# Turning rows for the gate as four-byte pairs instead of two-byte elements

## The chip, the core and the metric

The kernel runs on one core of a Trainium2 chip. The metric is the time of one execution on the device, in microseconds (us). The time before the change is 1499.75 us, the median of three runs (1499.15 to 1501.63).

## What is computed

Eight sequences of 2496 rows and 256 columns go through a Fourier transform along the rows, a complex product with a weight matrix, a soft threshold and the inverse transform. Each of the 19,968 resulting rows is then sent to the one of eight experts whose logit is largest, and the expert's output is scaled by the gate's probability. Cut to what matters:

```python
X = np.fft.rfft(x, axis=1)
Yr = Xr @ w_r - Xi @ w_i + b_r
Yi = Xr @ w_i + Xi @ w_r + b_i
Yr = np.sign(Yr) * np.maximum(np.abs(Yr) - lam, 0.0)   # Yi alike
y = np.fft.irfft(Yr + 1j * Yi, n=x.shape[1], axis=1)   # rows, 256 columns

logits = y @ w_gate                                    # 8 experts
expert_idx = np.argmax(logits, axis=1)
probs = softmax(logits)
h = np.maximum(y_sorted[lo:hi] @ w1[e], 0.0)           # per expert
out = gate_w[:, None] * (h @ w2[e])
```

## The kernel before, in words

**The transform stages.** A transform of 2496 points is split into one of 39 and one of 64 points, each a matmul with constants. For each of the eight batches: s1 (line 474) multiplies the rows of x by the first constant, and its result goes to DRAM (zd). Five groups follow: zload (line 492) brings z back, s2 (line 503) does the second transform, wmul (lines 531 to 533) the product with the weight matrix, thr and thr_sub (lines 540, 552) the threshold on VectorE, with ScalarE and GpSimd between them, inv1 (lines 579 to 581) the first half of the inverse, inv1_lo (line 591) its eviction, and vstore (line 596) the store to DRAM (vd). Nearly all products are made of two-byte halves: a value is kept as a high part and a low part in float16.

**From y to the gate.** The second half of the inverse runs on six chunks of a batch, five of four row groups and one of two. vload (line 622) brings v back, inv2 (line 632) multiplies, inv2_hi (ScalarE, line 639) and inv2_lo (VectorE, line 646) write a chunk's rows into yr: 128 rows on the partitions, and for each of four groups 256 high parts followed by 256 low parts. ytrans (VectorE, line 661) turns yr in squares of 32 by 32 elements into yt, so that columns of y come to lie on partitions. logits (TensorE, lines 674 and 676) then loads 128 columns of yt as weights, 16 times per chunk, and multiplies them with gd, the gate's weights in a block layout: the partition of gd is 32 q + i, and its block k holds the gate row that answers to the 32-wide square k. The first eight loads are of the high parts, the last eight of the low parts. route1 to route3 (from line 685) find the expert and the place of each row, and scatter (GpSimd, line 750) writes rows to their expert's list in DRAM.

**The experts.** A table (lines 854 to 909, VectorE) says which block of 256 rows is for which expert. It is made in parts as batches finish; the first part covers 12 blocks, needs batches 0 and 1 routed and all 16 weight matrices prepared (wprep, lines 768 to 807). fetch_w (lines 914, 922) and fetch_x (lines 928 to 933, with a transposing DMA) are issued on SyncE's queue, after SyncE has read the expert and the row from the table. post (lines 947, 950) reads the fetched tail on VectorE, up (lines 967 to 969) and down (lines 994 to 996) are the two matmuls of a block, down_store (line 1005) writes the result.

**What sets the order.** Every piece of work above is a task with an engine, a planned duration, a rank and dependences. A planner (class Plan) plays these through once when the program is built, and the order in which tasks start in that play is the order of the instructions on each engine's queue. Buffers of a pool are handed out in the same play. Batches 0 and 1 are routed early; from batch 2 on vload is held back to times 430, 520, ... of the play, so that the rest lies between expert blocks. Loads of expert weights for preparation are released at 40 + 26 u:

```python
ld = A("SP", 1.0, wprep_load, u, take=[wa], dma=3.4, rank=0.5, after=WT0 + WTD * u)
late = INV0 + INVD * (b - 2) if b >= 2 else 0.0
```

The planned duration of ytrans is 2.15 us for a full chunk.

Of the kernel before, what the change touches and what calls it, by code (L numbers as in the profile page):

```python
# [11 lines left out]
I32 = mybir.dt.int32  # L12
# [6 lines left out]
D = 256  # L19
# [233 lines left out]
def build(ctx: ExitStack, tc: tile.TileContext, x, w_r, w_i, b_r, b_i, wg, w1, w2,  # L253
# [3 lines left out]
    V, S, P, T, Q = nc.vector, nc.scalar, nc.gpsimd, nc.tensor, nc.sync  # L257
# [43 lines left out]
    wgs = cst.tile([128, 8, NE], F32, name="wgs")  # L301
# [17 lines left out]

    def load_g():  # L320
        for q in range(4):
            Q.dma_start(wgs[32 * q:32 * q + 32], wg.rearrange("(b i) e -> i b e", i=32))

    def load_cd():
        Q.dma_start(cd, c_d.rearrange("p (k m) -> p k m", k=K1))
# [329 lines left out]
    def ytrans(b, c):  # L655

        s = st[b]
        ns = min(4, SLOTS - 4 * c)
        yt = s[("yt", c)] = pool.tile([128, 4, 512], F16, name="yt", bufs=BUF["yt"])
        yt = s[("yt", c)] = yt.rearrange("p a b -> p (a b)").rearrange("p (k j t) -> p k j t", k=16, j=4)  # L660
        V.transpose(yt[:, :, :ns].rearrange("p k j t -> p j k t"),
                    s[("yr", c)][:, :ns, 0:2 * D].rearrange("p j (k t) -> p j k t", t=32))

    def logits(b, c):

        s = st[b]
        ns = min(4, SLOTS - 4 * c)
        yt = s.pop(("yt", c))
        o = lg[:32 * ns, c].rearrange("p h q e -> p (h q e)")
        for k in range(16):  # L670
            w = yt[:, k, :ns].rearrange("p j t -> p (j t)")
            g = gd[:, k % 8].rearrange("p h q e -> p (h q e)")
            if k < 8:
                T.matmul(o, w, g, start=(k == 0), stop=False)
            else:
                T.matmul(o[:, 0:32], w, g[:, 0:32], start=False, stop=(k == 15))
# [338 lines left out]
    A = L.add  # L1015
# [20 lines left out]
    i_w = A("SP", 1.0, load_w, rank=0, dma=1.8, take=[wu])  # L1036
    i_b = A("SP", 1.0, load_b, rank=0, dma=0.5)
    i_g = A("SP", 1.5, load_g, rank=0, dma=0.5)
    i_cd = A("SP", 0.6, load_cd, rank=0, dma=4.5)
    i_r = A("SP", 1.8, load_rest, rank=0.4, dma=2.0, after=26.0)  # L1040
# [19 lines left out]
    def ns_(c):  # L1060
        return min(4, SLOTS - 4 * c)
# [3 lines left out]
    for u in range(2 * NE):  # L1065
# [5 lines left out]
        for i in range(2):  # L1071
            m_ = A("DVE", 0.95, wprep_mul, u, i, deps=[scl], rank=1.2)
            h = A("ACT", 1.05, wprep_hi, u, i, deps=[m_], rank=1.2)
            l = A("POOL", 2.2, wprep_lo, u, i, deps=[h], rank=2, free=[wa])
# [4 lines left out]
    for b in range(B):  # L1079
# [3 lines left out]
        for c in range(6):  # L1083
            if b:
                ld.append(A("SP", 1.3, load_x, b, 4 * c, 4 * c + ns_(c), deps=[s1l[b - 1, c], nps[b - 1][c]],
                            rank=0.3, dma=8.0 * ns_(c) / 22))
# [9 lines left out]
        for c in range(6):  # L1096
            pb_, zb = L.buf("mm"), L.buf(("zt", "zt", "yt", "yt", "vs", "vs")[c] if b == 0 else "zt")
            k = ns_(c) / 4
            t = s1l[b, c] = A("PE", 1.72 * k, s1, b, c, deps=[ld[c], i_cc, nm] + ([s1l[b, c - 1]] if c else []),
                              rank=F - 9.5, take=[pb_, zb] + ([zdb] if not c else []))  # L1100
            l = A("ACT", 1.05 * k, s1_out, b, c, deps=[t], free=[pb_], rank=1)
# [3 lines left out]
        for i in range(5):  # L1105
            zs_, p2_, xa_, pw_, u_, cl_, sh_, pa_, vt_ = (L.buf(n) for n in ("zs", "mm", "xa", "mm", "u", "cl", "sh", "mm", "vt"))
            zl = A("SP", 1.2, zload, b, i, deps=sts, take=[zs_], free=[zdb], dma=11.8 / 5, rank=0)
            t = A("PE", 1.85, s2, b, i, deps=[zl, i_cd], take=[p2_, xa_], free=[zs_], rank=F + 3)
            h = A("ACT", 1.05, s2_hi, b, i, deps=[t, xs], rank=1)
            l = A("DVE", 1.28, s2_lo, b, i, deps=[h], free=[p2_], rank=1)  # L1110
            n_ = A("DVE", 0.5, s2_neg, b, i, deps=[l], rank=1)
            w = A("PE", 5.22, wmul, b, i, deps=[n_, wp_], take=[pw_, u_], free=[xa_], rank=F + 2)
# [8 lines left out]
            l = A("DVE", 1.28, inv1_lo, b, i, deps=[h], free=[pa_], rank=0)  # L1121
# [3 lines left out]
        pre = b < NPRE  # L1125
# [6 lines left out]
        for c in range(6):  # L1132
            k = ns_(c) / 4
            vs_, pb_, yr_, yt_ = (L.buf(n) for n in ("vs", "mm", "yr", "yt"))
            yrs.append(yr_)
            vl = A("SP", 0.6, vload, b, c, deps=vst + [i_z], take=[vs_], dma=9.1 * k / 5.5, rank=0.5 if pre else 2, after=late)
            t = A("PE", 1.3 * k, inv2, b, c, deps=[vl, i_r] + ([rt3["inv2", b - 1]] if b and not c else []),
                  take=[pb_, yr_], free=[vs_], rank=I + 2, lag=0.0 if pre else 6.0)
            h = A("ACT", 1.05 * k, inv2_hi, b, c, deps=[t, ys], rank=1 if pre else 1.5)
            l = A("DVE", 1.28 * k, inv2_lo, b, c, deps=[h], free=[pb_], rank=1 if pre else 1.5)  # L1140
            tks.append(A("POOL", 0.4, inv2_tok, b, c, deps=[h], rank=0.5))
            yt = A("DVE", 2.15 * k, ytrans, b, c, deps=[l], take=[yt_], rank=1 if pre else 1.4)
            lgs.append(A("PE", 0.5, logits, b, c, deps=[yt, gp_] + lgs[-1:] + ([rt3[b - 1]] if b else []), free=[yt_], rank=I + 1, lag=0.0 if pre else 2.0))
            if c == 5:
                rt3["inv2", b] = t
# [18 lines left out]
    def order(j):  # L1164

        d = [("d", j - 1, t) for t in range(2 if j <= NF else 1)] if j else []
        return [("u", j, 0)] + d + [("u", j, 1)] if j < NF else [("u", j, 0)] + d if j < NB else d
# [9 lines left out]
    for j in range(NB + 1):  # L1177
        o = order(j)
        seq += [o[i] for i in (0, 1, 3, 2)] if len(o) == 4 and j > js else o
    for j in range(NB):  # L1180
# [3 lines left out]
                       take=[xb_[j], tb_[j]], dma=1.95 if j < NF else 0.98, rank=1.2 + j * 1e-3, prev=ft.get(j - 1))  # L1184
        for w in range(2):
            wb_[j, w] = L.buf(f"wt{SLOT[j]}{w}")
            wl[j, w] = A("SP", 0.8, fetch_w, j, w, deps=[tabs[ep]] + (wdone if j < 2 else []) + ([sw] if j >= js else []),
                         take=[wb_[j, w]], dma=1.3, rank=1.1 + j * 1e-3 + w * 5e-4,
                         prev=wl.get((j - 1, w)))
    for k, (kind, j, q) in enumerate(seq):  # L1190
        if kind == "u":
# [3 lines left out]
            if q == 0:  # L1195
# [3 lines left out]
            t = ul[j, q] = A("PE", 2.65, up, j, q, deps=[ft[j], wl[j, 0], tb_["g", j][1]], take=[pb_, hb[j, q]],  # L1199
                             free=[xb_[j], wb_[j, 0]], rank=M + k)  # L1200
# [3 lines left out]
        else:  # L1204
            ob, pp = own("o", j), L.buf(f"po{q if j < NF else j % 2}")
            hs_ = [hb[j, i] for i in range(2 if j < NF else 1)]
            t = A("PE", 2.62, down, j, q, deps=[ul["o", j, i] for i in range(len(hs_))] + [wl[j, 1]], take=[pp],
                  free=hs_ + [wb_[j, 1]], rank=M + k)
# [23 lines left out]
```

## Time and profile before

| | us |
|---|---|
| median of three runs | 1499.75 |
| the profiled execution | 1501.02 |
| its span, first to last instruction | 1499.0 |
| TensorE busy in the span | 1402.3 |
| VectorE busy | 937.3 |
| ScalarE busy | 661.0 |
| GpSimd busy | 537.0 |

TensorE is PE in the rows, its weight loads PEld; VectorE is DVE, ScalarE ACT, GpSimd POOL, SyncE and its queue SP and SPq. The profiled execution is 1.3 us above the median. The mean granted clock of TensorE is 0.98 of full speed. The share of busy time is a mean over two different halves: up to about 541 us the transform stages run, after that mostly expert blocks. The table by stage in the section with the rows shows this.

### The profile page before, as it was taken

How to read it: one execution, taken by the hardware profiler on the slowest of the kernel's cores; microseconds unless marked ns; L12 is line 12 of the kernel's file. 1: busy time of each engine (PE TensorE's matmuls, PEld its weight loads, DVE VectorE, ACT ScalarE, POOL GpSimd, SP SyncE). 2: the span in 40 equal slices, each digit the busy share in tenths (PEclk: the TensorE clock that was granted, in tenths of full speed). 3: DMA queues.
4: the chain of work that ended last, by engine and by line, in shares of the span. 5: the costliest groups of instructions: out<-in, count | busy, mean ns of one | idle time of the engine just before them, and what ended most of it. 6: DMA issues, size and time to landing. Idle time of an engine off the chain costs nothing.

```text
span 1499.0 us, 33559 instructions
## 1 busy us (share of the span) xinstructions
PE 1402.3 (94%) x12850; PEld 1184.7 (79%) x12850; DVE 937.3 (63%) x1776; ACT 661.0 (44%) x869; POOL 537.0 (36%) x463
## 2 busy tenths in 40 slices
PE   5879888989887799999999999999999999999998
PEld 2668675767676578888888888888888888889997
DVE  2456788869686878666676666676666433343443
ACT  4667767766777444232333333323322222232222
POOL 0123314643564412643534525535435311111211
PEclk8999999999999899999999999999999999999999
DMA  8899978896899673874978988988678374676883
GB/s 258 246 287 290 267 231 266 254 314 177 265 289 262 176 196 81 228 197 108 308 219 249 256 240 248 226 232 239 187 228 230 81 233 115 188 201 205 213 210 104
DMA packets 229968, 330.00 MB, mean 220 GB/s; under 512 B 125109, under 2 KB 177623, under 8 KB 214960
## 3 DMA queue, kind: packets, MB, share of 16 engines
q1 hardware_dynamic: 213536, 286.78, 68.8%
q0 software_dynamic: 16272, 41.09, 8.1%
q8 instruction: 101, 1.65, 0.5%
q14 instruction: 59, 0.48, 0.1%
HBM read 276.61 MB, written 106.76 MB: 256 GB/s over the span
## 4 chain that ended last, share of the span: by engine, by line
PE 75%; DVE 9%; DMA 6%; issue 4%; ACT 3%; SPq 2%; POOL 1%; another core or an unknown queue 0%; POOLq 0%; ACTq 0%; DVEq 0%
PE pob L994 9%; PE mm L967 9%; PE pob L996 9%; PE mm L969 9%; PE mm L968 9%; PE pob L995 9%; PE mm L531 3%; PE mm L632 3%; PE mm L533 3%; PE mm L532 3%; PE mm L474 2%; DMA x<-x 2%; DVE vt L591 1%; PE mm L503 1%; DVE u L552 1%
## 5 line engine op out<-in xcount | busy, mean ns | idle before, releaser
L969 PE MATMUL mm<-xt,wt 128*128 128x256 f16 (+1 forms) x1472 | 367.0, 260 | 0.4 <-issue 0.2
L968 PE MATMUL mm<-xt,wt 128*128 128x256 f16 (+1 forms) x1472 | 367.0, 260 | 0.3 <-issue 0.3
L967 PE MATMUL mm<-xt,wt 128*128 128x256 f16 (+1 forms) x1472 | 367.1, 260 | 0.0
L1005 POOL DMA_INDIRECT out<-o,ix x163 | 176.5, 1083 | 512.5 <-ACT o L1001 415.0
L996 PE MATMUL pob<-wt,hh 128*128 128x256 f16 x1304 | 355.5, 273 | 2.1 <-issue 2.1
L994 PE MATMUL pob<-wt,hh 128*128 128x256 f16 x1304 | 355.4, 273 | 1.3 <-ACT o L1001 0.9
L995 PE MATMUL pob<-wt,hh 128*128 128x256 f16 x1304 | 355.4, 273 | 0.7 <-issue 0.7
L973 ACT ACTIVATE r<-mm 128x1024 f32<-128x1024 f32 x163 | 166.7, 1023 | 347.7 <-PE mm L969 293.4
L978 DVE CAST hh<-r 128x1024 f16<-128x1024 f32 x163 | 114.2, 700 | 252.5 <-ACT r L973 243.7
L750 POOL DMA_INDIRECT rows<-yr,ix x176 | 191.0, 1085 | 79.8 <-issue 60.7
L983 DVE TENSOR_TENSOR hh<-r,hh 128x1024 f16<-128x1024 f32 x163 | 199.8, 1226 | 5.5
L563 POOL TENSOR_TENSOR sh<-u,sh 128x1024 f16<-128x1024 f32 x40 | 86.7, 2168 | 291.3 <-ACT sh L558 283.2
L1001 ACT ACTIVATE o<-pob,g 128x256 f32<-128x256 f32 x163 | 76.4, 473 | 257.2 <-PE pob L996 248.5
L531 PE MATMUL mm<-w,xa 128*128 128x256 f16 x640 | 175.7, 275 | 9.3 <-DVE vt L591 4.6
L532 PE MATMUL mm<-w,xa 128*128 128x256 f16 x640 | 175.5, 274 | 0.0
L533 PE MATMUL mm<-w,xa 128*128 128x256 f16 x640 | 175.4, 274 | 0.0
L968 PEld LDWEIGHTS <-wt 128*128 128x128 f16 x1472 | 144.1, 98 | 15.9 <-issue 0.5
L967 PEld LDWEIGHTS <-wt 128*128 128x128 f16 x1472 | 144.0, 98 | 15.6
L969 PEld LDWEIGHTS <-wt 128*128 128x128 f16 x1472 | 144.0, 98 | 13.5 <-issue 0.5
L995 PEld LDWEIGHTS <-hh 128*128 128x128 f16 x1304 | 127.5, 98 | 17.6 <-issue 2.7
L996 PEld LDWEIGHTS <-hh 128*128 128x128 f16 x1304 | 127.5, 98 | 17.5 <-issue 2.0
L994 PEld LDWEIGHTS <-hh 128*128 128x128 f16 x1304 | 127.6, 98 | 16.4 <-issue 1.5
(172 smaller groups left out, 2073.0 us busy)
## 6 DMA issues: line engine op xcount, KB each, us to landing
wt<-wsc SPq DMA_DIRECT2D x184, 1024.0 KB
zs<-zd SPq DMA_DIRECT2D x80, 256.0 KB
vd<-vt SPq DMA_DIRECT2D x80, 256.0 KB
vs<-vd SPq DMA_DIRECT2D x40, 480.0 KB
x<-x SPq DMA_DIRECT2D x120, 156.0 KB
zd<-zt SPq DMA_DIRECT2D x37, 480.0 KB
wt<-moe_w SPq DMA_DIRECT2D x32, 512.0 KB
wsc<-wt SPq DMA_DIRECT2D x32, 512.0 KB
```

The source lines that it names most:

```text
L531: T.matmul(o, lh, w16[:, r, h, 0, :], start=(h == 0 and r == 0), stop=False)
L532: T.matmul(o, lh, w16[:, r, h, 1, :], start=False, stop=False)
L533: T.matmul(o, ll, w16[:, r, h, 0, :], start=False, stop=(h == 1 and r == 1))
L750: i = P.indirect_dma_start(out=rows, out_offset=bass.IndirectOffsetOnAxis(ap=s["ix"][:, j:j + 1], axis=0), in_=s[("yr", j // 4)][:, j % 4, ...
L967: T.matmul(pv[:, a, :], wh, xt[:, h, :], start=(h == 0), stop=False)
L968: T.matmul(pv[:, a, :], wh, xt[:, 2 + h, :], start=False, stop=False)
L969: T.matmul(pv[:, a, :], wl, xt[:, h, :], start=False, stop=(h == 1))
L983: V.tensor_tensor(hh[:, :, 1, :], H.pop(("r", j, q)).rearrange("p (a n) -> p a n", n=n), hh[:, :, 0, :], ALU.subtract)
L994: T.matmul(po, hi, wh, start=(fc == 0), stop=False)
L995: T.matmul(po, hi, wl, start=False, stop=False)
L996: T.matmul(po, lo, wh, start=False, stop=(fc == 7))
L1005: i = P.indirect_dma_start(out=out, out_offset=bass.IndirectOffsetOnAxis(ap=ix[:, t:t + 1], axis=0), in_=H.pop(("o", j, t)), in_offset=Non ...
```

## The change

The rows of y are turned as four-byte elements: two neighbours in a row, each of two bytes, stay together as one. A chunk has 1024 such elements per partition instead of 2048. After the turn, a partition of yt holds pairs, one of an even and one of an odd column of y. logits therefore takes every second element of yt as weights, the even ones for one matmul and the odd ones for the next, and the gate's rows are loaded in the order of the pairs. The planned duration of ytrans becomes 1.1 us.

```diff
     def load_g():
         for q in range(4):
-            Q.dma_start(wgs[32 * q:32 * q + 32], wg.rearrange("(b i) e -> i b e", i=32))
+            Q.dma_start(wgs[32 * q:32 * q + 32], wg.rearrange("(b i o) e -> i b o e", i=32, o=2))
...
-        yt = s[("yt", c)] = yt.rearrange("p a b -> p (a b)").rearrange("p (k j t) -> p k j t", k=16, j=4)
-        V.transpose(yt[:, :, :ns].rearrange("p k j t -> p j k t"),
-                    s[("yr", c)][:, :ns, 0:2 * D].rearrange("p j (k t) -> p j k t", t=32))
+        yt = s[("yt", c)] = yt.rearrange("p a b -> p (a b)").rearrange("p (k m o) -> p k m o", k=8, o=2)
+        V.transpose(yt.rearrange("p k m o -> p (k m o)").bitcast(I32).rearrange("p (k j t) -> p j k t", k=8, j=4)[:, :ns],
+                    s[("yr", c)][:, :ns, 0:2 * D].bitcast(I32).rearrange("p j (k t) -> p j k t", t=32))
...
         for k in range(16):
-            w = yt[:, k, :ns].rearrange("p j t -> p (j t)")
+            w = yt[:, k // 2, :32 * ns, k % 2]
             g = gd[:, k % 8].rearrange("p h q e -> p (h q e)")
...
-            yt = A("DVE", 2.15 * k, ytrans, b, c, deps=[l], take=[yt_], rank=1 if pre else 1.4)
+            yt = A("DVE", 1.1 * k, ytrans, b, c, deps=[l], take=[yt_], rank=1 if pre else 1.4)
```

The planned duration is one number, but the play goes differently from the first transposes on, and so does the order on every engine. Three places follow, each as it stands before and then after.

The first is SyncE's queue at the first expert fetch (xt and tl are a block's rows and their tails, rows the experts' lists in DRAM, zs the z of a group, vd and vs the store and load of v). Before:

```order
L931 DMA_TRANSPOSE xt_5404<-rows 128x4x256
L933 ISA
L933 DMA tl_5406<-rows 128x2x4
L928 TENSOR_LOAD tab_5298
L928 ISA x2
L931 ISA
L931 DMA_TRANSPOSE xt_5472<-rows 128x4x256
L933 ISA
L933 DMA tl_5474<-rows 128x2x4
L596 DMA vd_116<-vt 64x4x512 x2
L492 DMA zs<-zd_108 64x4x256 x2
```

After:

```order
L931 DMA_TRANSPOSE xt_5625<-rows 128x4x256
L933 ISA
L933 DMA tl_5627<-rows 128x2x4
L928 TENSOR_LOAD tab_5317
L928 ISA x2
L931 ISA
L931 DMA_TRANSPOSE xt_5658<-rows 128x4x256
L933 ISA
L933 DMA tl_5660<-rows 128x2x4
L622 DMA vs<-vd_112 120x1024
L622 DMA vs<-vd_113 120x2048
L596 DMA vd_117<-vt 64x4x512 x4
```

Ahead of the first L931 stand 76 of 80 loads of line 492 before and all 80 after; 66 of 80 stores of line 596 before and 72 after.

The second is TensorE at the first expert matmul (sm holds the logits, wt an expert's weights). Before:

```order
L676 LDWEIGHTS yt
L676 MATMUL sm<-gd,yt 128x32
L967 LDWEIGHTS wt_74
L967 MATMUL mm<-xt_5404,wt_74 128x256
L968 LDWEIGHTS wt_74
L968 MATMUL mm<-xt_5404,wt_74 128x256
```

After:

```order
L632 LDWEIGHTS cg
L632 MATMUL mm<-vs,cg 128x512
L967 LDWEIGHTS wt_74
L967 MATMUL mm<-xt_5625,wt_74 128x256
L968 LDWEIGHTS wt_74
L968 MATMUL mm<-xt_5625,wt_74 128x256
```

Ahead of the first L967 stand 304 of 320 matmuls of line 503, 576 of 640 of each of lines 531 to 533 and 140 of 160 of each of lines 579 to 581 before; after the change 320, 640 and 152.

The third is VectorE at its first expert instructions (g is made from the fetched tail tl and the table; u is the threshold's buffer). Before:

```order
L540 SCALAR_TENSOR_TENSOR u<-mm,bt 128x1024
L947 TENSOR_SCALAR g_5523<-tl_5406,tab_5298 128x2
L950 COPY ix_5525<-tl_5406 128x2
L591 SCALAR_TENSOR_TENSOR vt<-mm,vt 128x4x256
L552 SCALAR_TENSOR_TENSOR u<-u,sb,cl 128x1024
L947 TENSOR_SCALAR g_5565<-tl_5474,tab_5298 128x2
L950 COPY ix_5567<-tl_5474 128x2
L513 SCALAR_TENSOR_TENSOR xa<-mm,sb,xa 128x8x128 x2
L519 TENSOR_SCALAR xa<-xa 128x16x64 x2
L646 SCALAR_TENSOR_TENSOR yr<-mm,sb,yr 128x4x256
L661 STREAM_TRANSPOSE yt<-yr 128x4x16x32
```

After:

```order
L540 SCALAR_TENSOR_TENSOR u<-mm,bt 128x1024
L552 SCALAR_TENSOR_TENSOR u<-u,sb,cl 128x1024
L947 TENSOR_SCALAR g_5717<-tl_5627,tab_5317 128x2
L950 COPY ix_5719<-tl_5627 128x2
L513 SCALAR_TENSOR_TENSOR xa<-mm,sb,xa 128x8x128 x2
L947 TENSOR_SCALAR g_5741<-tl_5660,tab_5317 128x2
L950 COPY ix_5743<-tl_5660 128x2
L519 TENSOR_SCALAR xa<-xa 128x16x64 x2
L646 SCALAR_TENSOR_TENSOR yr<-mm,sb,yr 128x4x256
L591 SCALAR_TENSOR_TENSOR vt<-mm,vt 128x4x256
L661 STREAM_TRANSPOSE yt<-yr 128x4x8x32
```

Ahead of the first L947 stand 36 of 40 instructions of line 540 and 34 of 40 of line 591 before, 38 and 36 after.

## Rows read from the trace of the kernel before

**Rows 1.** The page: busy us, share of the span and instructions of each engine.

```profile
PE 1402.3 (94%) x12850; PEld 1184.7 (79%) x12850; DVE 937.3 (63%) x1776; ACT 661.0 (44%) x869; POOL 537.0 (36%) x463
```

**Rows 2.** Table by stage: stretch and length, busy us by engine, granted clock, DMA.

```profile
core 0: us, PE busy (x) PEld busy (x) DVE busy (x) ACT busy (x) POOL busy (x), PEclk, DMA share, GB/s
0.00:150.00 150.00, 120.51 (x778) 89.08 (x779) 71.70 (x163) 97.47 (x139) 26.32 (x17) 0.92 0.93 270
150.00:541.00 391.00, 333.95 (x2634) 258.51 (x2633) 306.95 (x536) 267.00 (x344) 172.11 (x116) 0.96 0.85 253
541.00:600.00 59.00, 58.68 (x586) 52.78 (x583) 48.13 (x92) 27.93 (x35) 13.15 (x11) 1.00 0.37 90
600.00:1100.00 500.00, 495.55 (x4755) 426.00 (x4753) 335.64 (x637) 156.62 (x201) 225.10 (x224) 1.00 0.82 225
1100.00:1499.00 399.00, 393.56 (x4110) 358.30 (x4107) 174.88 (x350) 112.00 (x151) 100.29 (x98) 1.00 0.65 182
```

**Rows 3.** VectorE by line and shape: busy us, mean ns of one, idle before.

```profile
L661 DVE STREAM_TRANSPOSE yt<-yr 128x2048 f16<-128x2048 f16 x40 | 92.3, 2309 | 1.1
L794 DVE TENSOR_SCALAR wt<-wt,wn 128x1024 f32<-128x1024 f32 x32 | 34.2, 1088 | 0.3
...
L661 DVE STREAM_TRANSPOSE yt<-yr 128x1024 f16<-128x1024 f16 x8 | 9.9, 1239 | 0.2
```

**Rows 4.** Transposes of line 661 by stage: stretch, busy us, count, clock, DMA.

```profile
150.00:541.00 391.00, 34.56 (x16) 0.96 0.85 253
...
600.00:1100.00 500.00, 64.01 (x30) 1.00 0.82 225
```

**Rows 5.** Waits from 150 to 541 us: who for whom, us, times, longest.

```profile
PE sm L601 <- ACT junk L570: 6.6, 3, 5.1
...
PE mm L531 <- DVE vt L591: 4.6, 2, 3.6
...
PE mm L579 <- issue: 0.2, 1, 0.2
...
ACT cl L546 <- DVE u L540: 34.2, 12, 7.6
```

**Rows 6.** The chain from 500 to 545 us (start, us, what), SyncE's wait, its load.

```profile
519.36 0.27 DVE tb L900
...
523.92 5.64 SPq L931
529.77 5.71 DMA tl<-rows
...
SPq L914 <- DVE tb L900: 10.1, 1, 10.1
...
535.48 2.03 SPq L492 DMA_DIRECT2D zs<-zd  x2
```

**Rows 7.** TensorE in order of time (start, us, line, shape): first expert matmul; lines 531 to 533.

```profile
541.30 0.27 PE L967 MATMUL mm<-xt,wt 128*128 128x256 f16 x1
...
555.00 0.27 PE L531 MATMUL mm<-w,xa 128*128 128x256 f16 x1
...
556.52 0.27 PE L533 MATMUL mm<-w,xa 128*128 128x256 f16 x1
```

**Rows 8.** Table by stage, the last 91 us before the first expert matmul.

```profile
450.00:541.00 91.00, 70.12 (x555) 55.02 (x554) 67.46 (x123) 51.59 (x63) 39.14 (x27) 0.91 0.82 235
```

**Rows 9.** Weight loads in order of time: a chunk's gate matmuls, and line 503.

```profile
1057.99 0.38 PEld L674 LDWEIGHTS <-yt 128*128 128x128 f16 x8
1058.30 0.28 PEld L676 LDWEIGHTS <-yt 128*128 128x128 f16 x8
1058.51 0.10 PEld L994 LDWEIGHTS <-hh 128*128 128x128 f16 x1
...
556.53 3.65 PEld L503 LDWEIGHTS mm<-cd,zs 128*128 128x128 f32 x32
560.10 0.10 PEld L579 LDWEIGHTS <-ce 128*128 128x128 f16 x1
```

## The prediction, made before the changed kernel ran

> **What bounds the kernel now.** I read the page first, then the stages, then the places where TensorE stands still, and last the chain of waits. The page gives TensorE 1402.3 us of work in a span of 1499.0 [rows 1]. In the table by stage [rows 2] the reader is to compare TensorE's busy time with the length of each stage. From 541 us on it is full: 58.68 of 59, 495.55 of 500, 393.56 of 399 us. Before that it is not: 333.95 of 391 us between 150 and 541, 57 us idle, at a mean granted clock of 0.96 of full. So a time saved on another engine after 541 us is worth nothing by itself, and what a change can win is the 57 us of idle time and the clock between 150 and 541, where the transform stages of batches 1 to 7 run. The 30 us idle in the first 150 us lie ahead of the first transpose.
>
> In that stretch VectorE is busy 306.95 of 391 us, 79% [rows 2], the most of any engine beside TensorE. The list of waits says who ended TensorE's pauses [rows 5]. It has 26 rows for TensorE, of which the first, the third and the last are shown; adding them by releaser gives VectorE 26.9 us, ScalarE 18.3, GpSimd 6.0, issue 4.3, TensorE itself 1.0. ScalarE for its part waits for VectorE most among its longer waits (34.2 us behind line 540). So 45.2 of 56.5 us, 80%, are at VectorE directly or one step behind it.
>
> The worst piece is its end. From 450 to 541 us TensorE works 70.12 of 91 us at a clock of 0.91 [rows 8]. The chain there [rows 6]: SyncE waits 10.1 us for the expert table, VectorE makes it until 519.6, the first expert fetch is issued at 523.92 and holds the queue for 5.64 us, its tail lands 5.71 us later, and VectorE, which waits for that tail, resumes at 535.5. The loads of z that batch 7 still needs stand behind that fetch and are issued at 535.48.
>
> **The change part by part.** *The transpose.* There are 48, one per chunk of a batch. A full one takes 2309 ns for 2048 two-byte elements per partition, the short one 1239 for 1024 [rows 3]. The difference is 1070 ns for 1024 elements, 1.045 ns each. With four-byte elements a full one has 1024, a short one 512. No row shows a four-byte transpose. Bounds: from below 1088 ns, the price of a four-byte VectorE instruction over 1024 elements [rows 3]; from above 2309 ns, if time goes by bytes. I take 1239 ns, the row with the same operation and count, and 1239 - 535 = 704 for the short one. Saving: 40 x 1.07 + 8 x 0.535 = 47 us of VectorE's 937.
>
> *Where it lies* [rows 4]. 16 transposes start between 150 and 541 us (14 full, 2 short): 14 x 1.07 + 2 x 0.535 = 16.1 us. The other 32, 30 of them between 600 and 1100 us, run beside a full TensorE, which covers them: nothing. Of the 16.1 us I count the 80% of idle time that hangs on VectorE: 12.8 us. The clock adds a little: 0.04 x 391 = 15.6 us of full-speed time are lost to it in this stretch, and if that loss shrinks with the idle time, 15.6 x 12.8 / 57 = 3.5 us come back. Together 16.3 us.
>
> *The order.* The plan is told 1.1 instead of 2.15 us for a transpose, so it places everything behind the first ones anew. I counted what stands ahead of the first expert matmul on TensorE (the second pair of order rows above). Before: 304 rows of line 503, 576 of each of lines 531 to 533, 140 of each of 579 to 581. After: 320, 640 and 152. The rows of lines 474, 632 and 674 are equally many. So 16 + 192 + 36 matmuls of the transform stages move ahead of the experts. At 112, 109 and 109 ns each (line 503: 32 loads from 556.53 to 560.10; lines 531 to 533: 14 steps from 555.00 to 556.52) [rows 7, 9] that is 1.8 + 20.9 + 3.9 = 26.7 us. The first expert block cannot come much earlier or later than now, at 541.3 [rows 7]: it waits for the table, which waits for the last expert's weights, whose loads are released by fixed times of the plan. If it starts at the same time, 26.7 us of work have gone into today's pauses and the end comes 26.7 us earlier. The queue of SyncE says how: all loads of z now stand ahead of the fetch (the first pair above), so batch 7 no longer waits for the 10.1 us, the 5.64 us and the landing. VectorE agrees: 38 of 40 rows of line 540 stand ahead of its first expert instruction, 36 before (the third pair).
>
> The two are not added: they are two views of one effect, of the VectorE time given free and of the TensorE work that uses it. I take their middle, 21.5 us.
>
> *Strided weights.* The gate's matmuls now load every second element of yt. Today 16 loads pass in 1058.51 - 1057.99 = 0.52 us, 32.5 ns each [rows 9]. No row shows a two-byte weight load with a step. From below it costs nothing; nothing excludes a small gain, but the matmuls they alternate with would hold them. From above it costs what loads with columns of four bytes take, 112 ns each at line 503 [rows 9], 79.5 ns more. I take zero: line 674's load has the same count of columns on the same partitions, and it is the nearest row. The Trainium skill speaks against it: its page TensorE: Matmul & The Clock Gate, section Weight-path perf modes, says that the fast load reads weights 32 bits at a time, two 16-bit ones, which with every second one unused would double 32.5 ns. The same table also calls its chunks "packed or strided"; no run here shows which holds. That rule is the third rival.
>
> *The rest.* The four loads of the gate weights stay four and of the same bytes (8 KB together), in 64-byte pieces instead of 32. They are issued in the first 20 us, where loads of x rule. Zero. The order of gate rows costs no instruction.
>
> **Sum.** The profiled execution took 1501.0 us: a span of 1499.0 and 2.0 around it. 1501.0 - 21.5 = 1479.5. The median of the runs is 1.3 us lower, so 1478.2; I say 1479, with bounds for this case from 16.3 to 26.7 + 3.5 us: 1470 to 1483, and up to 1489 if half of it is lost to other waits.
>
> **The rivals.**
> *The experts come later.* The first block slides by 10 to 18 us because the table or the last weights are placed later, and what is left is 3 to 11 us: 1489 to 1497. For it: VectorE's part of the table chain is planned anew and competes with more transform work. Against: the weights' release times are unchanged.
>
> *The four-byte transpose is no faster.* 2309 ns stay, the 16.3 us fall away, and an order made for short transposes meets long ones: of the 21.5 at most 5 us are left, or some 3 us are lost: 1495 to 1503. For it: no row shows the form. Against: the four-byte instruction of 1088 ns is as fast per element as two-byte ones.
>
> *Weight loads at twice the price* (the rule above). 40 full and 8 half chunks of 16 loads are 704 full loads, 15 chunk equivalents before 541 us and 29 after. 29 x 16 x 32.5 ns = 15 us fall on a full TensorE, all 704 make 23 us: 1501.0 - 1.3 - 21.5 + 15 to 23, 1493 to 1501. The step decides nothing until a load costs 21.5 / 704 = 30.5 ns more, 63 ns in all.
>
> *Weight loads at the price of four-byte columns*: the rival on the slower side. One mechanism, lines 674 and 676: 29 x 16 x 79.5 ns = 37 us on a full TensorE and up to 56 us in all, less 21.5: 1515 to 1534. It is slower than now from 63 ns a load. For it: the columns then lie four bytes apart as those of line 503 do. Against: line 503's 112 ns are also those of its matmuls, 32 in 3.65 us, so its loads alone may be cheaper.
>
> That the change does nothing can be ruled out only in part: the planned order differs on every engine from about batch 0's transposes on.
>
> **How the numbers follow.** Chances: forecast 0.65; experts later 0.13; transpose no faster 0.09; loads doubled 0.06; loads at the four-byte price 0.07. Faster and slower are counted from 0.2%, 3 us, about what a measurement of this kernel can tell from none. Faster: 0.65 + 0.13 + 0.03 + 0.01 = 0.82. Within: 0.04 of the transpose case and 0.04 of the doubled loads, 0.08. Slower: 0.07 + 0.02 + 0.01 = 0.10. The range 1470 to 1497 holds the forecast, the first rival and the near ends of the next two, 0.82; beyond it lie mainly the dear loads.
>
> **What would show it.** Line 661 as int32 at 1.24 us for 1024 elements and 55 us in all; above 1.5 us the first step is wrong. TensorE idle between 150 us and the first expert matmul down from 57 to about 35 us, and that matmul within 5 us of 541; if it comes after 550 the order step is wrong. VectorE no longer idle 3 us for the tail of the first fetch with transform work behind it. Line 674's loads 32 ns apart in the full stage; 60 or more would show the third or fourth rival. TensorE as full after the first expert block as now; new pauses there would be a wait that I have not named. What would make the forecast wrong as a whole is a pause of a new kind before 541 us, since an order of several hundred moved instructions can make one anywhere.

## The result, and the profile after

The changed kernel takes 1481.12 us, the median of four runs (1479.38 to 1482.12), beside 1499.45 us for the kernel before (1498.83 to 1501.63). The ratio is 0.9877, with a 95% interval of 0.9863 to 0.9890: 18 us faster. The forecast was 1479. The time was right; the split of the gain behind it was not, as the experiments show.

The page after, busy us and share of the span by engine, against [rows 1]:

```profile
span 1478.2 us, 33537 instructions
## 1 busy us (share of the span) xinstructions
PE 1401.3 (95%) x12850; PEld 1187.9 (80%) x12850; DVE 886.8 (60%) x1776; ACT 660.2 (45%) x869; POOL 532.3 (36%) x463
```

TensorE's work is the same to 1 us, and VectorE has lost 50.5 us, the 47 of the sum and a little more. The span is 20.8 us shorter, so nearly all that went is TensorE's idle time. The table by stage (stretch and length, busy us by engine, granted clock, DMA) against [rows 2]:

```profile
0.00:150.00 150.00, 121.26 (x781) 89.93 (x782) 73.30 (x164) 97.28 (x139) 26.78 (x17) 0.92 0.94 271
150.00:541.00 391.00, 348.89 (x2767) 274.80 (x2767) 297.33 (x543) 274.46 (x353) 177.02 (x117) 0.94 0.87 256
541.00:600.00 59.00, 59.00 (x577) 52.01 (x576) 44.33 (x108) 23.80 (x30) 15.33 (x14) 0.99 0.46 118
600.00:1100.00 500.00, 499.46 (x4815) 431.83 (x4814) 306.90 (x635) 159.07 (x205) 217.13 (x223) 1.00 0.81 230
```

Between 150 and 541 us TensorE is idle 42.1 us instead of 57.0, and between 600 and 1100 us 0.5 instead of 4.5. These two stretches give 18.9 of the 20.8 us. The granted clock in the first of them is lower, 0.94 instead of 0.96. From 600 to 1100 us VectorE has 28.7 us less to do, and that stretch has won no more than its 3.9 us of pauses. Even these are not shown to come from the change: profiled again as f1 below, the changed kernel has 5.6 us of pauses there, and e4 below, with the two-byte turn, has none.

The transposes by shape, against [rows 3]:

```profile
L661 DVE STREAM_TRANSPOSE yt<-yr 128x1024 int32<-128x1024 int32 x40 | 49.6, 1241 | 0.9
...
L661 DVE STREAM_TRANSPOSE yt<-yr 128x512 int32<-128x512 int32 x8 | 5.7, 710 | 0.2
```

A four-byte element costs what a two-byte element cost: 1241 ns for 1024 of them, as 1239 before. The weight loads of one chunk's gate matmuls, against [rows 9]:

```profile
1028.89 0.38 PEld L674 LDWEIGHTS <-yt 128*128 128x128 f16 x8
1029.21 0.28 PEld L676 LDWEIGHTS <-yt 128*128 128x128 f16 x8
1029.41 0.10 PEld L994 LDWEIGHTS <-hh 128*128 128x128 f16 x1
```

The 16 loads pass in 1029.41 - 1028.89 = 0.52 us, as before. At this pace, between the gate's matmuls, the step of two elements costs nothing.

The chain at the first expert fetch (start, us, what), against [rows 6]:

```profile
526.35 4.65 SPq L931
...
531.22 6.32 DMA tl<-rows
...
537.56 0.23 DVE g L947
```

The fetch, its landing and VectorE's wait for the tail (3.1 us, 3.0 before) are all still there, about two us later than before. And the first expert matmul, in the list of line 967 (first start after the durations), against [rows 7]:

```profile
L967 PE MATMUL mm<-xt,wt x1472: 218/273/283, 555.9 to 1466.9; 128*128 128x256 f16 x142, 128*128 128x128 f16 x42
```

It comes at 555.9 instead of 541.3.

### The profile page after: what moved, and what is told of

Same layout as the page of the kernel before. It is cut to its first block, busy times and chain, and to the rows that moved or that the text cites. A ratio compares the mean times of both kernels' runs of the same rounds, so it can differ in the third digit from the quotient of the medians.

```text
span 1478.2 us, 33537 instructions
## 1 busy us (share of the span) xinstructions
PE 1401.3 (95%) x12850; PEld 1187.9 (80%) x12850; DVE 886.8 (60%) x1776; ACT 660.2 (45%) x869; POOL 532.3 (36%) x463
## 4 chain that ended last, share of the span: by engine, by line
PE 74%; DMA 9%; DVE 8%; issue 4%; ACT 3%; SPq 2%; POOL 1%; POOLq 0%; ACTq 0%; DVEq 0%
PE mm L967 9%; PE mm L969 9%; PE mm L968 9%; PE pob L994 9%; PE pob L996 9%; PE pob L995 9%; DMA x<-x 3%; PE mm L531 3%; PE mm L532 3%; PE mm L533 3%; PE mm L632 3%; PE mm L503 2%; DMA zs<-zd 1%; PE mm L474 1%; DVE xa L513 1%
## 5 line engine op out<-in xcount | busy, mean ns | idle before, releaser
L967 PE MATMUL mm<-xt,wt 128*128 128x256 f16 (+1 forms) x1472 | 367.1, 260 | 0.0
L1005 POOL DMA_INDIRECT out<-o,ix x163 | 165.3, 1014 | 523.3 <-ACT o L1001 444.0
L750 POOL DMA_INDIRECT rows<-yr,ix x176 | 195.4, 1110 | 80.0 <-issue 59.7
L531 PE MATMUL mm<-w,xa 128*128 128x256 f16 x640 | 177.5, 277 | 7.4 <-DVE xa L513 2.6
L532 PE MATMUL mm<-w,xa 128*128 128x256 f16 x640 | 177.5, 277 | 0.0
L533 PE MATMUL mm<-w,xa 128*128 128x256 f16 x640 | 177.1, 277 | 0.0
L967 PEld LDWEIGHTS <-wt 128*128 128x128 f16 x1472 | 143.8, 98 | 15.1
L994 PEld LDWEIGHTS <-hh 128*128 128x128 f16 x1304 | 127.4, 98 | 15.7
```

The costliest lines, as they stand in the source:

```text
L531: T.matmul(o, lh, w16[:, r, h, 0, :], start=(h == 0 and r == 0), stop=False)
L532: T.matmul(o, lh, w16[:, r, h, 1, :], start=False, stop=False)
L533: T.matmul(o, ll, w16[:, r, h, 0, :], start=False, stop=(h == 1 and r == 1))
L750: i = P.indirect_dma_start(out=rows, out_offset=bass.IndirectOffsetOnAxis(ap=s["ix"][:, j:j + 1], axis=0), in_=s[("yr", j // 4)][:, j % 4, ...
L967: T.matmul(pv[:, a, :], wh, xt[:, h, :], start=(h == 0), stop=False)
L994: T.matmul(po, hi, wh, start=(fc == 0), stop=False)
```

## The experiments

Two things change at once: the device turns four bytes at a time, and the planner, told 1.1 instead of 2.15 us, puts out another order. Theory A is the sum of the prediction: VectorE's freed time is the gain, and the order is how TensorE uses it. Theory B is the rival that came up when the order was looked at: most of the gain is the order's own, and nearly any planned duration but 2.15 gives another one. Three groups of four kernels ran, each group on one chip with the kernel before beside it: 1497.95, 1507.55 and 1498.52 us there. Chips differ, so only ratios to the kernel before on the same chip are compared. The intervals are at 95%.

### The turn without the order, and the order without the turn

**e1_turn_only** is the changed kernel with one number put back:

```diff
-            yt = A("DVE", 1.1 * k, ytrans, b, c, ...
+            yt = A("DVE", 2.15 * k, ytrans, b, c, ...
```

> Four-byte turn, strided weights and reordered gate rows as in the changed kernel, but the planned duration left at 2.15 us, so that the order of all queues is that of before. Theory A (the freed VectorE time is the gain: 16 transposes before 541 us by about 1.07 us, 80% of it on the way to the end): 12 to 16 us faster than before, 1483 to 1488. Theory B (the new order is the gain, the freed time alone only shortens the four transposes that lie on the chain of waits, 8 us in all, to half): 3 to 5 us faster, 1494 to 1497, with the first expert matmul still near 541 us.

Measured: 0.9977 (0.9960 to 0.9993), 3.5 us faster; median 1493.84. The transposes take 1243 ns, and the order is that of before. This is theory B's figure, though the first expert matmul came at 533.7 us and not near 541.

**e2_order_only** is the kernel before with the same number set the other way:

```diff
-            yt = A("DVE", 2.15 * k, ytrans, b, c, ...
+            yt = A("DVE", 1.1 * k, ytrans, b, c, ...
```

> The kernel of before with only the planned duration set to 1.1 us: two-byte transposes of 2.31 us in the order of the changed kernel. Theory A: an order made for short transposes meets long ones and wins nothing, 1496 to 1503. Theory B: most of the gain is there, 10 to 15 us faster, 1484 to 1490, because the last loads of z stand ahead of the first expert fetch.

Measured: 0.9941 (0.9919 to 0.9962), 9 us faster; median 1487.84. The gain is just under theory B's 10 to 15 us. The order brings more than the freed time, with no instruction any cheaper: its transposes still take 2307 ns. The stretch from 150 to 541 us in e1 and then in e2 (columns as above):

```profile
150.00:541.00 391.00, 342.40 (x2718) 266.64 (x2717) 295.98 (x541) 270.15 (x347) 172.61 (x118) 0.95 0.85 256
```

```profile
150.00:541.00 391.00, 350.24 (x2784) 276.72 (x2782) 309.41 (x538) 274.75 (x355) 180.22 (x118) 0.95 0.86 257
```

With the old order and 11 us less of VectorE, TensorE is idle 48.6 us of the stretch (this is the fastest of e1's ten runs, 1486.5 us, 7 us below their median). With the new order and VectorE as busy as before, it is idle 40.8 us, less than in the changed kernel itself (42.1).

### What in the order it is

The prediction named two features: 26.7 us of transform work moved ahead of the first expert matmul, and the last loads of z moved ahead of the first expert fetch. e2 has both with the two-byte turn. The next two kernels keep that turn and come by other orders; by their traces each has the two features only in part.

**e4_before_plan_231** plans what the two-byte turn really takes:

```diff
-            yt = A("DVE", 2.15 * k, ytrans, b, c, ...
+            yt = A("DVE", 2.31 * k, ytrans, b, c, ...
```

> The kernel of before with the planned duration set to 2.31 us, what the trace shows for a two-byte transpose. Its order puts the same 640 rows of each of lines 531 to 533 ahead of the first expert matmul as the changed kernel's. Theory A: nothing on the device is cheaper, within 4 us of before, 1496 to 1503. Theory B: the order of before is the odd one out and any other wins, 8 to 15 us faster, 1484 to 1492.

Measured: 1.0016 (1.0002 to 1.0031); median 1498.83, theory A's figure. The expectation counts on 640 rows of line 531 ahead of the first expert matmul. The trace has 608 of them up to that matmul, which starts at 562.6 us (count, then durations, then first and last start):

```profile
L531 PE MATMUL mm<-w,xa x608: 269/273/421, 49.3 to 555.2; 128*128 128x256 f16 x152
```

The kernel before has 576, the changed kernel 640. Of the rows of line 579 it has 148, between 140 and 152. And the last four loads of z (76 of 80 are ahead) stand behind the first two expert fetches on SyncE's queue, as before:

```profile
525.25 5.22 SPq L931 DMA_TRANSPOSE xt<-rows  x1
...
536.70 2.62 SPq L492 DMA_DIRECT2D zs<-zd  x4
```

So e4 has half of the moved work of lines 531 to 533 and not the moved loads. It wins nothing, but it does not test the two features together.

**e5_before_z_first** holds the fetches back behind the last load of z:

```diff
-        fx = ft[j] = A("SP", 2.6, fetch_x, ..., deps=[tabs[ep], i_r] + ...
+        fx = ft[j] = A("SP", 2.6, fetch_x, ..., deps=[tabs[ep], i_r, zl] + ...
...
-            wl[j, w] = A("SP", 0.8, fetch_w, j, w, deps=[tabs[ep]] + ...
+            wl[j, w] = A("SP", 0.8, fetch_w, j, w, deps=[tabs[ep], zl] + ...
```

> The kernel of before, with one dependence more in the plan: the fetches of experts' rows and weights come after the last load of z. Up to about 500 us its order is that of before. If the z loads behind the first fetch are what cost the last 91 us before the experts (20.9 us of idle TensorE): 8 to 14 us faster, 1485 to 1492. If VectorE's time is what paces that stretch: within 4 us of before, 1496 to 1503, with the idle time only moved.

Measured: 1.0047 (1.0031 to 1.0064), 7 us slower; median 1502.9. Neither expectation has that. Its order has all 80 loads of z ahead of the first fetch, but again 608 and 148 rows of lines 531 and 579 ahead of the first expert matmul. SyncE's queue in order of time (start, us, line, transfer):

```profile
532.03 1.25 SPq L596 DMA_DIRECT2D vd<-vt  x2
536.14 1.25 SPq L492 DMA_DIRECT2D zs<-zd  x2
...
538.83 2.29 SPq L492 DMA_DIRECT2D zs<-zd  x2
...
546.98 8.99 SPq L931 DMA_TRANSPOSE xt<-rows  x1
```

No expert fetch stands ahead of these loads of z now, and still the first of them is issued at 536.14; in the kernel before, behind the fetch, it was 535.48 [rows 6]. The store of line 596 ahead of it is issued only at 532.03. So the fetch stood in front of the loads without holding them up. That explanation falls. The 7 us themselves say little: the edit issues the fetch 23 us later than before, and TensorE then stands still 4.9 us right before its first expert matmul, a pause that the kernel before does not have.

### Other planned durations for the four-byte turn

The second group ran on the slower chip. **f1_after_again** is the changed kernel itself.

> The changed kernel itself, beside the others on one chip. Against the order alone (0.9941) and the turn alone (0.9977), which multiply to 0.9918: if the two parts are independent, 0.990 to 0.993; if freed VectorE time is worth more under the new order, as the first measurement of the change (0.9877) says, 0.986 to 0.9895.

Measured: 0.9907 (0.9885 to 0.9930), 14 us. That does not tell independence (0.9918) from a larger joint effect.

**f2_plan_124** plans what the four-byte turn really takes:

```diff
-            yt = A("DVE", 1.1 * k, ytrans, b, c, ...
+            yt = A("DVE", 1.24 * k, ytrans, b, c, ...
```

> The changed kernel with the planned duration 1.24 us, the measured one, instead of 1.1. Its order has 76 of 80 loads of z ahead of the first expert fetch, as before, and 640 rows of line 531 ahead of the first expert matmul. If a true plan is worth something, the fastest of all, 1474 to 1480. If the loads of z behind the fetch cost what I thought, slower than the changed kernel by 5 us or more. If the order is a draw that these numbers move without meaning, anywhere from 1474 to 1490.

Measured: 0.9816 (0.9795 to 0.9836), 0.9 of a per cent below the changed kernel on this chip (1481.98 us against 1494.55). It has the last loads of z behind the first fetch, 76 of 80 ahead, and is the fastest kernel of the group: a second strike against that feature. It has 640 and 152 rows of lines 531 and 579 ahead of the first expert matmul, as f1 has.

**f3_plan_160** plans 1.6 us (the same line, `1.6 * k`).

> The changed kernel with the planned duration 1.6 us, in between the wrong old and the new one. If only the freed time counts, and any order but that of before uses it: 1477 to 1485, as the changed kernel. If a plan nearer to the truth is better: between the changed kernel and the turn in the old order, 1484 to 1490. If the order is a draw: anywhere from 1474 to 1490.

Measured: 0.9888 (0.9866 to 0.9910), the same as f1 within the intervals. It has 624 rows of line 531 ahead of the first expert matmul and 78 loads of z ahead of the first fetch.

**f4_plan_124_w24** takes the 1.24 of f2 and releases the loads of the expert weights earlier:

```diff
-INV0, INVD, WT0, WTD = 430, 90, 40, 26
+INV0, INVD, WT0, WTD = 430, 90, 40, 24
```

> As the last but one (planned duration 1.24 us), and the loads of expert weights for preparation released every 24 us instead of 26, so that the last weights, which the expert table waits for, are ready some 30 us earlier. If the table holds the experts back while TensorE is idle before them: faster than the changed kernel by 4 to 10 us, 1471 to 1477. If the transform stages' own waits set the idle time: within 4 us of it, 1477 to 1485, with the first expert matmul earlier and the same idle time in all.

Measured: 0.9915 (0.9894 to 0.9935), no better than f1 (within 4 us of it, as the second expectation has it) and 14 us slower than f2, which neither has. The table is made 31 us earlier than in f1, yet the first expert matmul starts at 558.0 us, nearly as late as in f1 (560.3). VectorE's table instruction in f1, in f4 and in f2:

```profile
523.02 0.26 DVE L900 TENSOR_TENSOR tb<-tb,t_True 128x96 f32<-128x96 f32 x1
```

```profile
491.52 0.26 DVE L900 TENSOR_TENSOR tb<-tb,t_True 128x96 f32<-128x96 f32 x1
```

```profile
490.67 0.26 DVE L900 TENSOR_TENSOR tb<-tb,t_True 128x96 f32<-128x96 f32 x1
```

f2 differs from f4 by the 24 alone and has the table as early, so the 24 did not bring it forward; the planned 1.24 had done that. What the 24 changed is the order: 624 rows of line 531 ahead of the first expert matmul instead of 640, 74 loads of z ahead of the first fetch instead of 76. The first expert matmul in f1 and then in f4 (in brackets the pause before it and what ended it, where there is one):

```profile
560.29 0.27 PE L967 MATMUL mm<-xt,wt 128*128 128x256 f16 x1
```

```profile
558.04 0.27 PE L967 MATMUL mm<-xt,wt 128*128 128x256 f16 x1 [0.54 <-DVE xa L513]
```

TensorE goes into its first expert matmul straight from the work ahead of it, in f4 after half a microsecond. So the table does not hold the experts back there; the order on TensorE's queue does, with the work that stands ahead.

### Two orders by two turns on one chip

The last group is a square: the orders made for 1.1 and for 1.24 us, each with the four-byte and the two-byte turn. g1 and g3 are the kernels of f1 and f2; g2 is that of e2; g4 is the kernel before with `1.24 * k`.

> The changed kernel (four-byte turn, planned 1.1 us) again, as one corner of a square of two orders and two turns on one chip. 0.987 to 0.991 of before.

> The same order with the two-byte turn (planned 1.1 us, 2.31 on the chip). If freed VectorE time is worth about 60% of the 16 us that lie before the experts under any order made for short transposes: 0.006 to 0.007 above the changed kernel on this chip, that is 9 to 11 us. If it is worth as little as under the old order: 2 to 5 us above it.

> The four-byte turn with the planned duration 1.24 us again. On the last chip it was 12.6 us faster than the changed kernel. If its order is the better one: again 8 to 15 us faster, 0.979 to 0.984 of before. If it was a matter of that chip: within 4 us of the changed kernel.

> The order of the last one with the two-byte turn. If freed VectorE time is worth a fixed share: 9 to 11 us above the kernel with the four-byte turn in this order, 0.986 to 0.991 of before. If an order made for 1.24 us needs it more or less than that made for 1.1: 3 us or 16 us above it, the two ends being what 16 transposes can give at least (the four on the chain of waits) and at most.

| | two-byte turn | four-byte turn | what the turn gives |
|---|---|---|---|
| order for 2.15 (first group) | 1 | e1 0.9977 (0.9960 to 0.9993) | 0.23%, 3.5 us |
| order for 1.1 | g2 0.9931 (0.9914 to 0.9948) | g1 0.9892 (0.9871 to 0.9913) | 0.39%, 6 us |
| order for 1.24 | g4 0.9870 (0.9843 to 0.9897) | g3 0.9861 (0.9841 to 0.9882) | 0.09%, 1 us |

Read down a column, the order is worth 0.7% (g2) and 1.3% (g4) with no cheaper instruction at all. Read along a row, the faster turn is worth 1 to 6 us, and in the last row it cannot be told from nothing. The intervals are too wide to tell the three rows apart. Of the expectations only g1's was met: g2's 6 us lie between its two, g3's distance from g1 too, and the turn's 1 us in g4 is less than either end. g4, whose transposes take 2.31 us as ever, is as fast as the changed kernel. Between 1.1 and 1.24 with the four-byte turn, g3 was 4.7 us below g1 in the medians, with intervals that overlap; f2, the same kernel as g3, was 12.6 us below f1, clear of them. It has the lowest median on either chip.

In these two orders the waits show that the pauses belong to the order. These are TensorE's longest from 150 to 541 us (who for whom, us, times, longest), in g3 with the four-byte turn and then in g4 with the two-byte turn:

```profile
PE mm L632 <- DVE xa L513: 6.1, 1, 6.1
PE mm L474 <- DVE xa L513: 5.8, 5, 3.0
PE sm L601 <- ACT junk L570: 4.6, 2, 3.6
PE mm L531 <- DVE xa L519: 4.4, 4, 2.0
PE mm L531 <- DVE xa L513: 3.2, 2, 2.2
```

```profile
PE mm L474 <- DVE xa L513: 5.8, 5, 3.0
PE sm L601 <- ACT junk L570: 4.6, 2, 3.6
PE mm L632 <- DVE xa L513: 4.4, 2, 4.0
PE mm L531 <- DVE xa L519: 4.4, 4, 2.0
PE mm L531 <- DVE xa L513: 3.2, 2, 2.2
```

Four of the five lines are the same to the tenth, and all of them together come to 41.7 and 42.0 us, though VectorE is busy 307.7 us of the stretch in the one and 316.8 in the other. The changed kernel and e2, which share the other order, have 41.9 and 40.6 us. Under the old order it is otherwise: the kernel before has 56.5 us of such pauses and e1 47.9, though e1's profile is of its fastest run.

## Why the prediction was right, and where it was not

**What bounds the kernel: right.** Of the 20.8 us, 15.7 came out of TensorE's pauses ahead of the first expert matmul. The 33 transposes that now run after 541 us won nothing that can be told from the spread between executions.

**The price of the turn: right.** 1241 and 710 ns against 1239 and 704. **The strided weights: right**, 32.5 ns a load. The Trainium skill (TensorE: Matmul & The Clock Gate, Weight-path perf modes) says that a fast load reads weights 32 bits at a time, two 16-bit ones. That a step would double the price was the prediction's own inference from it; the 0.52 us for 16 loads in the changed kernel does not bear the inference out.

**What the freed time is worth: the term that was mis-sized.** The step counted 80% of 16.1 us, 12.8, and 3.5 us of clock on top, because 80% of TensorE's pauses ended on VectorE or one engine behind it. Measured at a fixed order it is 3.5 us under the old one (interval 1 to 6), 6 and 1 under two others. The share of pauses that an engine ends is not the share of its saved time that arrives. A likely reason, which no run isolates, is that a pause that ends on line 513 or 591 stays as long as that instruction is late, whatever a transpose elsewhere in the queue takes. The changed kernel's own list fits that: VectorE still ends 25.4 us of pauses (26.9 before), while ScalarE's fell from 18.3 to 13.6, GpSimd's from 6.0 to 2.9 and issue from 4.3 to 0. The price that e1's expectation took from the chain of waits of before was nearer: four transposes stand on that chain between 150 and 541 us, 8 us in all, and halving them gives 4.

```profile
201.11 2.27 DVE yt L661
277.71 2.31 DVE yt L661
298.11 2.22 DVE yt L661
349.40 1.15 DVE yt L661
```

TensorE's longest pauses after, from 150 to 541 us, against [rows 5]:

```profile
PE mm L579 <- DVE vt L591: 5.5, 2, 4.4
PE mm L579 <- ACT zt L481: 5.4, 3, 4.8
PE sm L601 <- ACT junk L570: 3.6, 1, 3.6
PE mm L579 <- DVE xa L513: 3.5, 2, 3.3
...
PE sm L674 <- DVE yt L661: 0.8, 1, 0.8
```

Only the last line is a wait for a transpose itself.

**The clock: gave nothing.** It was to give 3.5 us back. The granted mean from 150 to 541 us went from 0.96 to 0.94, though TensorE was idle less. In f1 and g1, the same kernel again, it is 0.96, so a loss is not shown either.

**The order: too large, because the experts did come later.** The step counted 26.7 us; the order alone is worth 9 or 10. The prediction said itself that a first expert matmul after 550 us would show the step wrong, and it came at 555.9. The work that moved is even a little more than was counted: a matmul of line 503 has two rows in the trace, so the 16 of them are 3.6 us and not 1.8, 28.5 in all, and TensorE's busy time ahead of the first expert matmul went from 454.8 to 485.1 us, 30.3 more. Of these, 15.7 went into pauses (86.5 us of idle time ahead of that matmul became 70.9), and by the other 14.6 the matmul slid. From that matmul to the end the span is 35.4 us shorter, 31.3 of work and 4.1 of pauses.

Of the two features that the step rested on, the place of the loads of z is not what makes the difference: f2 and g4 lack it and are the fastest of their turns, and e5, which has it, wins nothing. The work moved ahead of the experts is not refuted. At the two-byte turn the orders with 640 rows of line 531 ahead of the first expert matmul (e2, g2, g4) are all faster than before, by 0.6 to 1.3%, and those with 608 (e4, e5) are not. At the four-byte turn 624 (f3, f4) cannot be told from f1's 640. The idle time ahead of the first expert matmul goes with it: 86.5 us in the kernel before, 84.6 and 86.5 in e4 and e5, 79 in f3 and f4, 70 to 76 in all profiles with 640 rows; but it is also 77 in e1, which has 576 and the four-byte turn. No run moves this work and nothing else, so that it is the cause is not shown.

**Two views of one effect: wrong.** The order and the turn each give something without the other. With e2 and e1 the order gives 9 us and the turn 3.5; on the third chip 10 and 6. The prediction had 26.7 and 16.3 for them, both too large, and did not add them; the middle of two terms that are too large, 21.5, stood beside a measured gain of 18. That the time came out is luck to that extent. The change itself was worth 18, 14 and 16 us in its three measurements.

**What stays open.** Which feature of an order makes it good was not isolated. It is not the place of the loads of z, not an early table by itself (f4 has one), and not a true planned duration as such: 2.31 is true for the two-byte turn and wins nothing, 1.24 is false for it and wins 1.3%. Transform work ahead of the experts goes with the gain but does not explain f2 beside f1, which have equal counts of it. Of the 9 us between their profiled spans, 5.2 are TensorE's own busy time, 1400.3 against 1405.5 us for as many instructions, at a mean granted clock of 0.980 against 0.976; whether the order raises the clock was not tested. TensorE takes its instructions in the planned order, and which of them finds its input late differs from order to order. The order of before was one of the poorer ones: of four other planned durations, three (1.1, 1.24, 1.6) were faster at each turn that they ran with, and 2.31 was no faster. No attempt was made to measure the gate row loads by themselves.

## What to carry to other kernels

When a planner with durations makes the order, changing one duration is a second edit beside the one on the device: run each alone before either gets the credit. Price a cheaper instruction by the pieces of it on the chain of waits, not by the share of pauses that its engine ends; here the first would have said 4 us, the second 13, and 1 to 6 were measured. Where the order is that sensitive (0.987 to 1.002 from one number, at the same two-byte turn), trying a few values of it on the chip was worth more than the edit. And count in each run's own trace the feature that an order is meant to have: e4's did not have what was expected of it.

## What the runs showed of the hardware

In these shapes a transpose on VectorE goes by elements and not by bytes: 512 more four-byte elements cost 531 ns (710 to 1241) and 1024 more two-byte ones 1070 (1239 to 2309), 1.04 ns each in both. Weight loads of every second two-byte element pass at the same 32.5 ns as dense ones, in the gate's matmuls. The kernel before took 1497.95, 1507.55 and 1498.52 us on three chips, a spread as large as the order's effect, which is why only ratios on one chip were used.
